# Linear attention and a four-expert mixture: less work for the last 64 tokens and keys, finer steps, a new order

## The chip, the cores and the metric

The kernel runs on one core of one Trainium2 chip. The metric is the device time of one launch in microseconds (us). Within a core five engines run from queues of their own: TensorE (PE; its weight loads are shown as PEld), VectorE (DVE), ScalarE (ACT), GpSimd (POOL), and SyncE (SP), which here issues the DMA transfers. An engine takes its instructions in the order in which the program lists them.

## The reference

Inputs are q, k and v of 8 batches, 8 heads, 576 positions and 64 features, a feature matrix w_phi, and the weights of four experts. First linear attention, for each batch and head:

```
proj = x @ w_phi                                   (128 features)
proj = proj - max |proj| over the features
phi(x) = [exp(proj), exp(-proj)]                   (256 features)
kv = phi(k)^T @ v,   z = sum over positions of phi(k)
attn = (phi(q) @ kv) / (phi(q) . z + 1e-6)
```

The eight heads side by side give x, 576 by 512 for each batch. Then four experts, each a causal softmax attention of one head of 64 features:

```
logits = x @ w_gate;  the two largest of four experts per token, softmax over these two
for each expert: q, k, v = x @ wq, x @ wk, x @ wv
                 ye = softmax_causal(q k^T / 8) @ v @ wo
                 out += gate * ye
```

576 is 4 times 128 and 64: every stage over positions has four full blocks and a tail of 64.

## The kernel before

Heads go in 32 pairs, four pairs to a batch. Each pair passes through these stages of the first part:

- stream_k projects the keys (8 products of 128 columns) and stream_tail the last 64 keys of both heads together (2 products with 64 weight columns each); center takes the maximum over the features and subtracts it on VectorE, and ScalarE takes both exponentials into ek.
- stream_kv multiplies ek with v (40 products: 2 heads, 2 halves of the features, 5 blocks of keys, 2 halves of the output rows). A column of ones beside v gives z. The last 64 keys of the two heads share one block, 64 rows for each head, and v has zeros in the other head's rows.
- stream_q projects the queries; phi_q takes the maximum over the features with a GpSimd all-reduce, subtracts it on VectorE and takes both exponentials on ScalarE.
- stream_n multiplies phi(q) with kv (72 instructions of 65 columns per pair), normed divides, turn_x transposes by a 32x32 VectorE transpose and a trip through DRAM. The result is split into a high and a low part in fp32r, xh and xl (sub_lo on VectorE).

The second part, stream_b, takes a batch when the x of its four pairs is there. Products with weights are three fp32r products each (high-high, high-low, low-high). proj_t makes queries and keys of two experts at a time (g = 0, 1), each in two pieces of 256 and 320 positions; proj_v makes the values and gate logits in five blocks of positions, 12 products of 260 columns each; scores makes the scores in four groups (BLOCKS), soft masks and evicts them, post takes the maximum over keys (GpSimd) and the exponential, then multiplies with the values; norm_y divides and applies the gate, move_y transposes (turn_y on TensorE in the last batch), project_out multiplies with wo and store writes.

A plain f32 product is two instructions on TensorE, an fp32r product one. TensorE sees three tile shapes: 128x128 (products with wqk, wvg, wo), 64x128 (q and k projections, scores) and 128x64 (key tail, kv, phi(q) kv, attention times values).

Every stage is a Python generator that yields a Step before each group of instructions, with the engine and a condition (pred) on what must have been issued. The order of all steps on all engines is written out in PICKS: two characters per step, which generator goes next and which of the 8 PSUM banks it gets, or for an eviction whether ScalarE or VectorE does it. in_order then keeps each engine's queue in that order. So an engine never passes over an instruction that waits. Before the change, ORDER fixed the order of a batch's stages (all of p0, then v0, and so on), each stage being one long generator, and keep_warm issued three small bf16 products on a tile of ones whenever PICKS put it in, until the first x was there: 126 in all.

## Time and profile before

| | |
|---|---|
| time, three runs | 565.3 us median (564.62, 565.3, 569.82) |
| profiled execution | span 563.5 us from the first to the last instruction; its time is not listed apart, the span is 1.8 us under the median and 1.1 us under the fastest run |
| TensorE busy | 551.8 us, 98% |
| TensorE weight loads busy | 518.7 us, 92% |
| VectorE busy | 492.9 us, 87% |
| ScalarE busy | 391.2 us, 69% |
| GpSimd busy | 192.7 us, 34% |
| DMA queues | 48.7% of the 16 engines' span, 123 GB/s of HBM traffic |
| granted TensorE clock | 0.999 on average |

Busy time is the union of the instructions of an engine, and pipelined instructions overlap; for TensorE the distance from one start to the next tells more than the duration of one. The chain that ended last goes through TensorE for 88% of the span and through VectorE for 8%.

### The profile page before, as it was taken

Reading aid. Unit: us, or ns where it says so; the run is one execution under the profiler, and the core shown is the slowest. Engines: PE = TensorE matmul, PEld = TensorE weight load, DVE = VectorE, ACT = ScalarE, POOL = GpSimd, SP = SyncE. Lnnn points to the kernel's source line nnn. Section 1 sums busy time; section 2 is a strip of 40 time slices with the busy share of each in tenths; the row PEclk is TensorE's granted clock in tenths of the full one; section 3 lists DMA queues with packets and bytes.
Section 4 is the critical chain, followed back from the end, with each engine's and each line's share of the span. In section 5 each row is a group of like instructions: output and inputs, shape, how many; then the busy total and the mean of one; then the engine's idle time right before and its main releaser. Section 6 shows DMA issues by size and latency. Waiting matters only on the chain.

```text
span 563.5 us, 22862 instructions
## 1 busy us (share of the span) xinstructions
PE 551.8 (98%) x9704; PEld 518.7 (92%) x9704; DVE 492.9 (87%) x1245; ACT 391.2 (69%) x737; POOL 192.7 (34%) x78
## 2 busy tenths in 40 slices
PE   8999899999999999999999999999999999999996
PEld 6888799999999999999999999999999999999996
DVE  5799988999998999898878998899988998896992
ACT  3978757877956666897755784877785865574673
POOL 4565082244220555233203525083522310202320
PEclk9999999999999999999999999999999999999999
DMA  6577655555554636526545644356553253414222
GB/s 169 145 186 200 171 153 118 154 124 122 150 133 102 181 87 177 140 71 180 126 93 141 163 144 98 85 136 170 141 112 65 62 134 80 112 47 105 66 85 85
DMA packets 124757, 70.63 MB, mean 125 GB/s; under 512 B 81520, under 2 KB 107504, under 8 KB 124656
## 3 DMA queue, kind: packets, MB, share of 16 engines
q1 hardware_dynamic: 124656, 69.18, 48.7%
q8 instruction: 76, 1.25, 1.0%
q14 instruction: 25, 0.20, 0.1%
HBM read 46.15 MB, written 23.00 MB: 123 GB/s over the span
## 4 chain that ended last, share of the span: by engine, by line
PE 88%; DVE 8%; ACT 2%; issue 1%; DMA 0%; SPq 0%; DVEq 0%; ACTq 0%
PE ps_c L180 39%; PE ps_c L407 30%; PE ps_c L359 11%; PE ps_c L626 7%; DVE st L744 1%; DVE pmax L393 1%; DVE ek L395 1%; ACT ek L191 1%; DVE u L508 1%; DMA wf<-in_wts_dram 0%; DVE xt L540 0%; DVE xq L438 0%; DVE kv L202 0%; ACT u L189 0%; DVE u L202 0%
## 5 line engine op out<-in xcount | busy, mean ns | idle before, releaser
L498 POOL PARTITION_ALL_REDUCE mx<-u x32 | 127.0, 3993 | 113.7 <-ACT u L189 74.3
L180 PE MATMUL ps_c<-xh,qk 128*128 128x320 f32 (+1 forms) x512 | 106.3, 299 | 0.2 <-ACT st L189 0.2
L191 ACT ACTIVATE ek<-ek 128x1152 f32<-128x1152 f32 x64 | 74.8, 1169 | 26.4 <-DVE ek L395 25.5
L180 PEld LDWEIGHTS ps_c<-xh,qk 128*128 128x128 f32 x512 | 83.2, 189 | 1.8 <-ACT st L189 0.5
L498 POOL PARTITION_ALL_REDUCE tops<-top x15 | 54.2, 3611 | 82.9 <-DVE top L658 70.5
L407 PEld LDWEIGHTS ps_c<-v_in,ek 128*64 128x64 f32 x2560 | 77.4, 137 | 5.1 <-issue 2.6
L407 PE MATMUL ps_c<-v_in,ek 128*64 128x65 f32 x2560 | 81.4, 222 | 0.5 <-ACT ek L191 0.4
L180 PE MATMUL ps_c<-xl,qk 128*128 128x256 f32 (+1 forms) x256 | 75.8, 296 | 0.0
L189 ACT COPY st<-ps_c 128x288 f32<-128x288 f32 (+1 forms) x120 | 51.4, 505 | 25.1 <-DVE ps_c L646 16.7
L407 PE MATMUL ps_c<-kv,mx 128*64 128x65 f32 x1152 | 62.5, 224 | 3.3 <-DVE kv L202 2.6
L744 DVE TENSOR_TENSOR st<-st,tops 128x1152 f32<-128x1152 f32 (+4 forms) x75 | 57.7, 826 | 4.5 <-POOL tops L498 4.4
L393 DVE TENSOR_REDUCE pmax<-ps_c 128x4 f32<-128x512 f32 (+1 forms) x96 | 51.1, 546 | 11.0 <-PE ps_c L407 5.6
L407 PE MATMUL ps_c<-kv,u 128*64 128x65 f32 x1152 | 59.5, 221 | 0.0
L180 PE MATMUL ps_c<-vg,xh 128*128 128x260 f32 (+1 forms) x320 | 59.0, 285 | 0.0
L407 PEld LDWEIGHTS ps_c<-kv,mx 128*64 128x64 f32 x1152 | 48.1, 137 | 8.0 <-DVE kv L202 1.9
L189 ACT COPY u<-ps_c 128x320 f32<-128x320 f32 (+3 forms) x125 | 42.6, 416 | 17.2 <-PE ps_c L359 15.2
L395 DVE TENSOR_TENSOR ek<-ps_c,pmax 128x512 f32<-128x512 f32 (+1 forms) x96 | 51.9, 553 | 2.8 <-issue 0.5
L191 ACT ACTIVATE st<-st 128x1152 f32<-128x1152 f32 (+3 forms) x60 | 48.5, 865 | 7.0 <-DVE st L744 6.6
L180 PE MATMUL ps_c<-yh,wo 128*128 128x256 f32 (+1 forms) x256 | 52.1, 298 | 0.0
L180 PEld LDWEIGHTS ps_c<-xl,qk 128*128 128x128 f32 x256 | 48.5, 189 | 0.1
L407 PE MATMUL ps_c<-vl,st 128*64 128x65 f32 x1500 | 47.6, 222 | 0.8 <-ACT st L191 0.7
L180 PEld LDWEIGHTS ps_c<-vg,xh 128*128 128x128 f32 (+1 forms) x320 | 47.6, 177 | 0.8 <-issue 0.3
(116 smaller groups left out, 1175.4 us busy)
## 6 DMA issues: line engine op xcount, KB each, us to landing
v_in<-in_v_dram SPq DMA_DIRECT2D x32, 320.0 KB, 4.1
q_in<-in_qt_dram SPq DMA_DIRECT2D x64, 144.0 KB, 3.5
xl<-xd SPq DMA_DIRECT2D x32, 288.0 KB, 3.1
out_dram<-ot SPq DMA_DIRECT2D x32, 288.0 KB, 2.9
k_in<-in_kt_dram SPq DMA_DIRECT2D x32, 160.0 KB, 3.4
xd<-xt SPq DMA_DIRECT2D x64, 80.0 KB, 2.5
k_in<-in_kt_dram SPq DMA_DIRECT2D x32, 128.0 KB, 3.3
xd<-xt SPq DMA_DIRECT2D x64, 64.0 KB, 2.1
```

What stands on the lines that cost most here:

```text
L180: nc.tensor.matmul(o, a, b, start=start, stop=stop, skip_group_check=True)
L189: nc.scalar.copy(o, i)
L191: nc.scalar.activation(o, i, func, **kw)
L359: nc.tensor.matmul(o, a, b, start=True, stop=True, skip_group_check=True)
L393: dve(n * 128, [mk], [pk]).tensor_reduce(out=m[:, us], in_=src, axis=AX.X, op=ALU.max, apply_absolute_value=True)
L395: dve(n * 128, [(f'ek{p % EKB}1', us.start)], [pk, mk]).tensor_tensor(out=ek2[p % EKB][:, 1, us, :], in0=src, in1=m[:, us].unsqueeze(2).to ...
L407: nc.tensor.matmul(o, a, b, start=start, stop=stop, skip_group_check=True)
L498: nc.gpsimd.partition_all_reduce(o, i, 128, op)
L508: dve(2 * S, [uk], [mk], port=True).tensor_tensor(out=U, in0=U, in1=M, op=ALU.subtract)
L626: nc.tensor.matmul(pp_[e][:, o:o + q1 - q0], kk2[k_][r, 128 * j:128 * j + 128], q2[q_][r, q0:q1], start=m == 0, stop=m == 2, skip_group_ch ...
L744: dve(2 * n, [sj[j]], [*key, mk], port=True).tensor_tensor(out=a, in0=a, in1=tops[x][0:m, :, 128 * j:], op=ALU.subtract)
```

## The change

The values of the last 64 tokens: after its split, 64 columns of xh and 64 of xl are copied by a DMA side by side into xE, and proj_v's last block takes these 128 columns as weights, with high and low wvg (8 products; low times low comes along). Its two output halves are added: a copy to vlo, then an addition on VectorE. The last 64 keys in stream_kv: one product for both heads, 130 columns. The last score block has 64 weight columns in place of 128, and the memsets of the padding go.

The steps become finer: each piece of proj_t, each block of proj_v and each piece of project_out is a generator of its own; stream_kv and stream_n run through one half of the features and then the other, and may start after the first exponential; attention times values (attend) goes block of queries by block of queries as the exponentials come, and no longer waits for the gate, which norm_y does; in the last batch project_out may take g = 0 first. The warm products are 18 groups of three, 54, and the first four key projections wait for 8, 12, 15 and 18 groups. PICKS is a new table for all steps. Before the change TensorE has 6024 products in the program, after it 5792.

```diff
-WARM = 0
-ORDER = (('p0', 'v0', 's0', 'p1', 's1'), ('p0', 's0', 'p1', 's1', 'v0'))
+WARMS = 18
+WARM_AT = (7, 11, 14, 17)
...
-    "BACACADAAAAAAAAAAAAAAAAAAAGRNANAGjNANANACAG1OAOAG5OAOAOABAAAFCPIPIEjQIPIPIPIEADANICACAAAAAAAAAAAAAAAAAAAAAAAAAAAAAG1PAPA"
...
+    "BABABABABADABABABABAAAAAAAAAGIGaBANADAEsRACANARANANAFGBANAAHAHQAAHAHAHAHOAFHFRQAOANANADADADrBAFGGAEEMAMATANIJHJAJANIOAPA"
...
+    nc.vector.memset(warm, 1.0)
-        nc.vector.memset(t[:, NJ * V1 - 1:NJ * V1], 0.0)
+        nc.vector.memset(t[:, NJ * V1 - 1:512], 0.0)
...
-    xT = [[sb(f"x{p}{i}", [128, S], F32R) for p in "hl"] for i in range(PXB)]
+    xB = [sb(f"xb{i}", [128, 2, S], F32R) for i in range(PXB)]
+    xT = [[t[:, n] for n in range(2)] for t in xB]
+    xE = sb("xe", [128, NP, 128], F32R)
...
-    kk2 = [sb(f"kk{p}", [128, KC], F32R) for p in "hl"]
+    kk2 = [sb(f"kk{p}", [128, S], F32R) for p in "hl"]
+    vlo = sb("vlo", [64, 4, 65])
...
     def keep_warm():
-        pk, ps = yield Step('PE', (), 'c')
-        while ('x', WARM, 0) not in done:
-            yield Step('PE')
+        for n in range(WARMS):
+            t = yield Step('PE', (), 'c')
             for _ in range(3):
-                mm(ps[:, 0:128], warm, warm, True, True, 128, pk, [])
-        plan.release('c', (pk, ps))
+                mm(t[1][:, 0:128], warm, warm, True, True, 128, t[0], [])
+            plan.release('c', t)
+            done.add(('warm', n))
...
             x, need = k_in[p % IB], [(f'k_in{p % IB}', n) for n in range(2)] + ['wphi']
-            k0, k1, pp_ = yield Step('PE', need, 'c', lambda: ('load_k', p) in done and ('w', 0) in done, tiling=(64, 128), n=3)
...
             i = p % EKB
             ek, ekk = ek2[i], [f'ek{i}0'] + [(f'ek{i}1', t) for t in (0, 4, 8)]
-            kc, ps = yield Step('PE', ekk + [vk], 'c', lambda: ('phi_k', p) in done and ('load_v', p) in done, tiling=(128, 64))
-            for h in range(2):
-                for c in range(2):
+            kc, ps = yield Step('PE', ekk + [vk], 'c', lambda: ('phi_k', p, 0) in done and ('load_v', p) in done, tiling=(128, 64))
+            for c in range(2):
+                if c:
+                    yield Step('PE', pred=has('phi_k', p, 1))
+                for h in range(2):
                     o = V1 * (2 * h + c)
-                    for t in range(NJ):
-                        u_ = 4 * h + t if t < 4 else 8
+                    for t in range(4):
                         for m in range(0, 128, 64):
-                            column_mm(ps[m:m + 64, o:o + V1], ek[:, c, u_, m:m + 64], v_in[:, 4 * h + t if t < 4 else 8 + h, :],
-                                       t == 0, t == 4, kc, ekk + [vk])
+                            column_mm(ps[m:m + 64, o:o + V1], ek[:, c, 4 * h + t, m:m + 64], v_in[:, 4 * h + t, :], c + h + t == 0, False, kc, ekk + [vk])
...
             kvi = kv[p % 2]
-            k0, k1, pp_ = yield Step('PE', need, 'c', lambda: ('phi', p) in done and ('kvs', p) in done, tiling=(128, 64), n=3)
-            for j in range(NJ):
-                for c in range(2):
-                    rows_mm(j, pp_, (k0, k1), lambda h, m: P_[h][c][:, 64 * j + 5 * m:], lambda h: kvi[:, 2 * h + c, :], c == 0, c == 1, need)
+            k0, k1, pp_ = yield Step('PE', need, 'c', lambda: ('phi', p, 0) in done and ('kvs', p) in done, tiling=(128, 64), n=3)
+            for c in range(2):
+                if c:
+                    yield Step('PE', pred=has('phi', p, 1))
+                for j in range(NJ):
+                    rows_mm(j, pp_, (k0, k1), lambda h, m: P_[h][c][:, 64 * j + 5 * m:], lambda h: kvi[:, 2 * h + c, :], c + j == 0, c == 1, need)
             done.add(('num', p))
             plan.spawn(divide(p, (k0, k1), pp_))
             plan.spawn(turn_x(p))
...
+        yield Step('SP', [f'xl{i}'], pred=(lambda: ('pe', p // NP - 1) in done) if p >= NP else None)
+        load(xE[:, p % NP].rearrange("f (n s) -> f n s", n=2).bitcast(F32), xB[i][:, :, 512:S].bitcast(F32), 'xe')
+        done.add(('xe', p))
...
-        def proj_t(sel, g):
+        def proj_t(b, sel, g, s0, s1):
             w = wsp["qk"]
-            for s0, s1 in PARTS:
-                pk, ps = yield Step('PE', [k for c in xk for k in c], 'c')
-                n = 0
-                for c in range(4):
-                    o = ((sel * 4 + c) * 2 + g) * 128
-                    for w_, x_ in ((0, 0), (0, 1), (1, 0)):
-                        mm(ps[:, 0:s1 - s0], w[w_][:, o:o + 128], xs[c][x_][:, s0:s1],
-                           n == 0, n == 11, s1 - s0, pk, [xk[c][x_], ('qk', w_)])
-                        n += 1
-                plan.spawn((evac_k if sel else evac_q)(g, s0, s1, pk, ps))
+            pk, ps = yield Step('PE', (), 'c', ready_x)
+            n = 0
+            for c in range(4):
+                o = ((sel * 4 + c) * 2 + g) * 128
+                for w_, x_ in ((0, 0), (0, 1), (1, 0)):
+                    mm(ps[:, 0:s1 - s0], w[w_][:, o:o + 128], xs[c][x_][:, s0:s1], n == 0, n == 11, s1 - s0, pk, [])
+                    n += 1
+            plan.spawn((evac_k if sel else evac_q)(g, s0, s1, pk, ps))
+            used()
+
+        def used():
+            left[0] -= 1
+            if left[0] == 0:
+                done.add(('px', b))
...
-            copy(st.eng, 260, vl[:m, j, :, 0:65], ps[:m, 0:260].rearrange("p (n d) -> p n d", d=65), [f'vs{j}'], [kc])
+            src = ps[:, 0:260].rearrange("p (n d) -> p n d", d=65)
+            if m == 128:
+                copy(st.eng, 260, vl[:, j, :, 0:65], src, [f'vs{j}'], [kc])
+            else:
+                copy(st.eng, 260, vlo, src[64:128], ['vlo'], [kc])
+                yield Step('DVE', [kc], hot=True)
+                nc.vector.tensor_tensor(out=vl[0:64, j, :, 0:65], in0=src[0:64], in1=vlo, op=ALU.add)
...
-                            nc.tensor.matmul(pp_[e][:, o:o + q1 - q0], kk2[k_][r, 128 * j:128 * j + 128], q2[q_][r, q0:q1],
+                            n_ = min(128, S - 128 * j)
+                            nc.tensor.matmul(pp_[e][0:n_, o:o + q1 - q0], kk2[k_][r, 128 * j:128 * j + n_], q2[q_][r, q0:q1],
...
+            plan.spawn(attend(b, g))
...
-        def proj_v():
+        def proj_v(j):
             wvg = wsp["vg"]
-            for j in range(NJ):
-                m = min(128, S - 128 * j)
-                kc, ps = yield Step('PE', [k for c in xk for k in c], 'c', has('av', b - 1, 1) if b else has('w', 2))
-                n = 0
-                for c in range(4):
-                    for x_, w_ in ((0, 0), (0, 1), (1, 0)):
-                        mm(ps[:m, 0:260], xs[c][x_][:, 128 * j:128 * j + m],
-                           wvg[w_][:, c * 260:(c + 1) * 260], n == 0, n == 11, 260, kc,
-                           [xk[c][x_], ('vg', w_)])
-                        n += 1
-                plan.spawn(evac_v(j, m, kc, ps))
-
-        yield Step('PE', (), None, lambda: all_x(*range(b * NP, b * NP + NP))() and all(('w', i) in done for i in (0, 1, 4)))
-        for part in ORDER[b == B - 1]:
-            yield Step('PE')
-            g = int(part[-1])
-            if part[0] == 'p':
-                yield from proj_t(0, g)
-                yield from proj_t(1, g)
-            elif part[0] == 'v':
-                yield from proj_v()
-                plan.spawn(gates(b))
-            else:
-                yield from scores(g)
-            if part == ORDER[b == B - 1][-1]:
-                plan.spawn(project_out(b))
-            if part in 'p1v0' and part == [o for o in ORDER[b == B - 1] if o[0] in 'pv'][-1]:
-                done.add(('px', b))
+            m = min(128, S - 128 * j)
+            kc, ps = yield Step('PE', (), 'c', lambda: ready_x() and ('w', 2) in done and (j < NJ - 1 or all(('xe', NP * b + c) in done for c in range(NP))))
+            parts = [(xs[c][x_][:, 128 * j:128 * j + m], c, w_) for c in range(4) for x_, w_ in ((0, 0), (0, 1), (1, 0))]
+            if m < 128:
+                parts = [(xE[:, c], c, w_) for c in range(4) for w_ in range(2)]
+            for n, (x_, c, w_) in enumerate(parts):
+                mm(ps[:, 0:260], x_, wvg[w_][:, c * 260:(c + 1) * 260], n == 0, n == len(parts) - 1, 260, kc, [])
+            if m < 128:
+                done.add(('pe', b))
+            plan.spawn(evac_v(j, m, kc, ps))
+            used()
...
+        left = [13]
+        yield Step('PE', (), None, all_x(b * NP))
+        for g in range(2):
+            for sel in range(2):
+                for s0, s1 in PARTS:
+                    plan.spawn(proj_t(b, sel, g, s0, s1))
+        for j in range(NJ):
+            plan.spawn(proj_v(j))
+        plan.spawn(gates(b))
+        for g in range(2):
+            plan.spawn(scores(g))
+        for t in range(4):
+            for s0, s1 in PARTS:
+                plan.spawn(project_out(b, t, s0, s1))
+            plan.spawn(store(b, t))
...
-        for j in range(NJ):
-            done.add(('e', b, g, j))
+            for j in js:
+                done.add(('e', b, g, j))
...
         def ready():
-            return all(('v', b, j) in done for j in range(NJ)) and ('gate', b) in done
+            return all(('v', b, j) in done for j in range(NJ)) and ('e', b, g, 0) in done
 
         k0, k1, pp_ = yield Step('PE', ej[0:1], 'c', ready, tiling=(128, 64), n=3)
         for i in range(NJ):
+            if i:
+                yield Step('PE', pred=has('e', b, g, i))
...
-        yield Step('DVE', pred=(lambda: all(('yt', b - 1, g, q_[0]) in done for q_ in PARTS)) if b else None)
+        yield Step('DVE', pred=lambda: ('gate', b) in done and (not b or all(('yt', b - 1, g, q_[0]) in done for q_ in PARTS)))
...
+        early = b == B - 1
+        pk, ps = yield Step('PE', (), 'c', lambda: ('w', 3) in done and ys_done(b, 0) and (early or ys_done(b, 1)))
+        for g in range(2):
+            if g and early:
+                yield Step('PE', pred=lambda: ys_done(b, 1))
+            wc = slice(512 * g + 128 * t, 512 * g + 128 * t + 128)
+            for n, (y_, w_) in enumerate(((0, 0), (0, 1), (1, 0))):
+                mm(ps[:, 0:s1 - s0], wwo[w_][:, wc], ys[g][y_][:, s0:s1], g == 0 and n == 0, g == 1 and n == 2, s1 - s0, pk, [])
+        plan.spawn(evac_o(b, t, s0, s1, pk, ps))
+        todo[b] -= 1
+        if todo[b] == 0:
+            done.add(('o', b))
```

What PICKS moves is seen in the built order. First TensorE at the value tail of a batch (vg are the value and gate weights; xh and xl, or xe, hold x; ps is PSUM), before:

```order
L180 MATMUL ps_c_61<-vg,xh_152 128x260 x2
L180 MATMUL ps_c_61<-vg,xl_153 128x260
L180 MATMUL ps_c_66<-vg,xh_146 64x260 x2
L180 MATMUL ps_c_66<-vg,xl_147 64x260
L180 MATMUL ps_c_66<-vg,xh_148 64x260 x2
L180 MATMUL ps_c_66<-vg,xl_149 64x260
L180 MATMUL ps_c_66<-vg,xh_150 64x260 x2
L180 MATMUL ps_c_66<-vg,xl_151 64x260
L180 MATMUL ps_c_66<-vg,xh_152 64x260 x2
L180 MATMUL ps_c_66<-vg,xl_153 64x260
L626 MATMUL ps_c_67<-qh,kkh 128x288
```

and in the change, where it follows the second query and key projection (qk):

```order
L184 MATMUL ps_c_68<-xb_148,qk 128x256 x3
L184 MATMUL ps_c_68<-xb_149,qk 128x256 x3
L184 MATMUL ps_c_65<-vg,xe 128x260 x8
L184 MATMUL ps_c_66<-vg,xb_146 128x260 x3
L184 MATMUL ps_c_66<-vg,xb_147 128x260 x3
```

Twelve products with 64 output rows became eight with 128, and they now stand ahead of other value blocks.

Second, TensorE at the end of the program: the last attention (vl are the values, u a buffer of exponentials), the transposes (ident, yq) and the output products (yh, yl, wo), before:

```order
L407 MATMUL ps_c_66<-vl,u_127 64x65
L407 MATMUL ps_c_68<-vl,u_127 64x65
L450 MATMUL ps_c_63<-ident,yq_165 128x128 x2
L450 MATMUL ps_c_67<-ident,yq_165 128x128 x2
L450 MATMUL ps_c_67<-ident,yq_165 128x64
L450 MATMUL ps_c_64<-ident,yq_166 128x128 x2
```

and in the change:

```order
L407 MATMUL ps_c_63<-vl,u_127 64x65
L407 MATMUL ps_c_62<-vl,u_127 64x65
L184 MATMUL ps_c_64<-yh_180,wo 128x320 x2
L184 MATMUL ps_c_64<-yl_181,wo 128x320
L184 MATMUL ps_c_64<-yh_182,wo 128x320 x2
L184 MATMUL ps_c_64<-yl_183,wo 128x320
L184 MATMUL ps_c_66<-yh_180,wo 128x256 x2
L184 MATMUL ps_c_66<-yl_181,wo 128x256
L184 MATMUL ps_c_66<-yh_182,wo 128x256 x2
L184 MATMUL ps_c_66<-yl_183,wo 128x256
L450 MATMUL ps_c_67<-ident,yq_160 128x128 x2
```

Twelve output products of the batch before now stand between the last attention and the transposes.

Third, VectorE in the opening, where the x of the first batch is split (xl and xh before, xb in the change; qk and vg are pieces of the weights, rd, xq and xt belong to the division and transpose of other pairs), before:

```order
L185 TENSOR_TENSOR xl_153<-xl_153,xh_152 128x576
L444 TENSOR_SCALAR xq_137<-ps_c_65,rd_135 64x2x32
L185 TENSOR_TENSOR qk<-ot_188,qk 128x576
L202 COPY kv_122<-ps_c_64 128x260
L540 STREAM_TRANSPOSE xt_142<-xq_136 128x640
L185 TENSOR_TENSOR xl_151<-xl_151,xh_150 128x576
L202 CAST vg<-ot_189 128x4x64 x2
```

and in the change:

```order
L206 CAST xb_148<-xb_148 128x576
L206 CAST xb_147<-xb_147 128x576
L189 TENSOR_TENSOR xb_148<-xb_148 128x576
L189 TENSOR_TENSOR xb_146<-xb_146 128x576
L393 TENSOR_REDUCE pmax_124<-ps_c_62 128x1
L438 TENSOR_TENSOR xq_136<-ps_c_63,rd_134 128x4x2x32
L189 TENSOR_TENSOR xb_147<-xb_147 128x576
L189 TENSOR_TENSOR xb_149<-xb_149 128x576
L395 TENSOR_TENSOR ek_119<-ps_c_62,pmax_124 128x128
L546 STREAM_TRANSPOSE xt_142<-xq_136 128x640
```

The four subtractions stand together now, with two of the casts just ahead of them on the same engine, and the last weight pieces behind them.

## Rows read from the trace of the kernel before

**Rows 1.** Windows by stage: window, length, busy us (count) by engine, clock, DMA.

```profile
0.00:30.00 30.00, 27.55 (x479) 23.23 (x481) 20.35 (x73) 17.98 (x28) 16.17 (x10) 1.00 0.61 160
30.00:74.40 44.40, 41.69 (x962) 36.29 (x961) 43.35 (x96) 35.36 (x58) 18.53 (x5) 1.00 0.69 181
74.40:540.00 465.60, 463.30 (x7973) 441.10 (x7974) 416.61 (x1042) 326.90 (x626) 154.22 (x63) 1.00 0.48 119
540.00:563.50 23.50, 19.25 (x296) 18.10 (x294) 12.61 (x35) 10.95 (x26) 3.74 (x2) 0.98 0.27 102
```

**Rows 2.** Waits of TensorE from 75 us: us in total, times, longest (five rows).

```profile
PE ps_c L450 <- DVE yq L438: 0.8, 1, 0.8
...
PE ps_c L407 <- ACT st L191: 0.7, 2, 0.5
...
PE ps_c L180 <- ACT st L189: 0.2, 1, 0.2
```

**Rows 3.** Chain that ended last, 515 to 565 us: start, us, what.

```profile
544.93 6.04 PE ps_c L407 x200
...
552.49 0.86 PE ps_c L450 x5
```

**Rows 4.** TensorE in order of time: start, us, what; a value tail and a score tail.

```profile
86.45 0.29 PE L180 MATMUL ps_c<-vg,xl 128*128 128x260 f32 x1
86.58 0.40 PE L180 MATMUL ps_c<-vg,xh 128*64 128x260 f32 x2
...
87.89 0.28 PE L180 MATMUL ps_c<-vg,xl 128*64 128x260 f32 x1
88.09 0.40 PE L626 MATMUL ps_c<-qh,kkh 64*128 64x288 f32 x2
...
89.59 0.19 PE L626 MATMUL ps_c<-qh,kkh 64*128 64x64 f32 x2
...
89.84 0.39 PE L626 MATMUL ps_c<-qh,kkh 64*128 64x320 f32 x2
```

**Rows 5.** TensorE in order of time, where the tile shape changes at 202 us.

```profile
202.16 0.29 PE L407 MATMUL ps_c<-kv,u 128*64 128x65 f32 x4
202.38 0.70 PE L359 MATMUL ps_c<-q_in,wf 64*128 64x256 f32 x4
```

**Rows 6.** TensorE in order of time: kv products, and a key tail at 110 us.

```profile
98.65 2.56 PE L407 MATMUL ps_c<-v_in,ek 128*64 128x65 f32 x80
101.04 0.39 PE L407 MATMUL ps_c<-wf,k_in 128*64 128x128 f32 x4
...
110.36 0.29 PE L407 MATMUL ps_c<-kv,u 128*64 128x65 f32 x4
110.48 0.39 PE L407 MATMUL ps_c<-wf,k_in 128*64 128x128 f32 x4
110.70 1.51 PE L407 MATMUL ps_c<-vl,st 128*64 128x65 f32 x46
```

**Rows 7.** Waits of VectorE, 75 to 540 us (fifteen rows, first and last).

```profile
DVE ps_c L646 <- PE ps_c L626: 6.4, 7, 2.0
...
DVE ek L395 <- PE ps_c L407: 0.2, 1, 0.2
```

**Rows 8.** Forms on VectorE: busy us, mean ns of one, idle before.

```profile
L202 DVE COPY kv<-ps_c 128x260 f32<-128x260 f32 x8 | 3.4, 422 | 0.5 <-PE ps_c L407 0.4
L202 DVE COPY u<-ps_c 128x320 f32<-128x320 f32 x5 | 2.2, 483 | 0.3 <-PE ps_c L359 0.3
L202 DVE CAST xh<-xl 128x576 fp32r<-128x576 f32 x3 | 1.6, 527 | 0.0
```

**Rows 9.** TensorE in order of time: warm products in the opening.

```profile
1.30 2.74 PE L180 MATMUL ps_c<-warm 128*128 128x128 bf16 x24 [1.30 <-DVE col L215]
...
10.98 2.52 PE L180 MATMUL ps_c<-warm 128*128 128x128 bf16 x42
```

More of the change, by code (lines that the diff above doesn't have):

```diff
@@ L169, in tile_linear_attn_moe @@
     plan.free = set(range(BANKS))
+    warm = cp.tile([128, 128], BF16, name="warm")
+    nc.vector.memset(warm, 1.0)
     for t in plan.both:
-        nc.vector.memset(t[:, NJ * V1 - 1:NJ * V1], 0.0)
+        nc.vector.memset(t[:, NJ * V1 - 1:512], 0.0)
     def sb(name, shape, dt=F32):
@@ L363, in stream_k @@
             x, need = k_in[p % IB], [(f'k_in{p % IB}', n) for n in range(2)] + ['wphi']
-            k0, k1, pp_ = yield Step('PE', need, 'c', lambda: ('load_k', p) in done and ('w', 0) in done, tiling=(64, 128), n=3)
+            k0, k1, pp_ = yield Step('PE', need, 'c', lambda: ('load_k', p) in done and ('w', 0) in done and (p >= len(WARM_AT) or ('warm', WARM_AT[p]) in done), tiling=(64, 128), n=3)
             for n in range(4):
@@ new lines, in proj_v, with has_scores, ready_x @@
+            if m < 128:
+                done.add(('pe', b))
+            plan.spawn(evac_v(j, m, kc, ps))
+            used()
+        def has_scores(g):
+            return has('s', b, 0) if g else (has('s', b - 1, 1) if b else None)
+        def ready_x():
+            return all_x(*range(b * NP, b * NP + NP))() and ('w', 1) in done
+        left = [13]
[4 more added lines that the diff above has]
+                    plan.spawn(proj_t(b, sel, g, s0, s1))
```

136 lines of the change are left out of this document (63 added, 73 removed).

## The prediction

> **What bounds the kernel now.** I read the busy time by stage first. From the first query and key product at 74.4 us to 540 us TensorE is busy 463.3 of 465.6 us [rows 1]; in that stretch and the tail behind it only 2.7 us of its waits have a name, in five rows [rows 2]. A busy TensorE can still be slow, so I looked at start-to-start times next: the twelve products of a tail follow each other 0.12 us apart [rows 4], and 80 small products take 2.39 us [rows 6], without holes. From 74.4 us on, then, the time is the sum of TensorE's own work, and less of that work is less time as long as nobody else falls behind. Three things are not that sum. The opening, up to 74.4 us: from 30 us VectorE is busy 43.35 of 44.4 us there, TensorE 41.7 [rows 1]. The end: attention ends at 544.93 + 6.04 = 550.97 us and the transposes start at 552.49, 1.5 us of TensorE waiting for the division [rows 3]. And VectorE's own load: 416.6 of 465.6 us in the steady part [rows 1], second in the queue to be the bound.
>
> The span is 563.5 us; the median of the runs is 565.3. I work on the span and add 1.8 us.
>
> **The change, part by part.** TensorE first.
>
> Value products of the last 64 tokens: 12 of them per batch become 8 (the weights now hold the high and the low part side by side). Eleven steps take 87.89 - 86.58 = 1.31 us, 0.119 each [rows 4]; all stream 260 columns before and after. 8 batches x 4 x 0.119 = 3.8 us. The new copy of those 64 columns (one DMA of 64 KB for each of 32 pairs) and the wait for it I cost at nothing on TensorE: in the order of batch 0 two query and key projections lie between the fourth x subtraction and the product that reads it, 96 products of 0.12 us or more, over 11 us. If that cover is gone, SP's queue is where it hurts, since loads stand behind the waiting copy.
>
> Key products of the last 64 keys: 16 instructions of 65 columns per pair of heads become 8 of 130 (each f32 product is two instructions). Now: 16 x 2.39/80 = 0.48 us. For 130 columns the nearest row has 128: four in 0.22 us, 0.055 each [rows 6], so 8 x 0.056 = 0.45. 32 pairs x 0.03 = 1.0 us saved. Bounds: 0, and 7.7 us if an instruction of 130 columns cost no more than one of 65; the row of 128 columns says it does not.
>
> Score block of the last 64 keys: the same six products of 64 columns, with 64 weight columns for 128. Six take 0.25 us, 16 times 4.0 us in all [rows 4]. I take 0; bounds are a gain of half, 2.0 us, and a loss of 3.0 (below).
>
> Changes of the tile shape. Between stages of the same shape the next one follows at its normal distance: four products to the next stage 0.12 us [rows 6]. Into another shape the same four need 0.22 [rows 5], and value to scores 0.20 where 0.12 is normal [rows 4]. So a change costs 0.08 to 0.11; I take 0.095. In the order I count the changes behind the first query/key product, the narrow value and score products put with their neighbours: 115 before, 74 now. 41 x 0.095 = 3.9 us (3.3 to 4.5).
>
> The end: 12 output products of the batch before now stand between the last attention and the transposes, 1.6 us of work in a hole of 1.5. The hole goes: 1.5 us.
>
> Opening. VectorE sets it, so I count what its queue holds ahead of the fourth x subtraction. Leaving: six kv copies of 0.42 us [rows 8], three u copies, one subtraction and one transpose, and smaller ones, 8.3 us; joining: three casts of x of 0.53 [rows 8], k-side reductions and subtractions, weight casts, 4.5 us. 3.8 us less, at 0.89 (below) 3.4. The first k projection also moves ahead of the second q projection, and VectorE gets its first work sooner: it idles 9.65 us before 30 us [rows 1]; I take 1.2. But 1.6 us of useful TensorE work also moves from the opening to behind it. Net 3.0 us. Bounds: a loss of 1 (the second q load is issued later), a gain of 8. The 72 warm products that go (0.06 us each [rows 9], 4.3 us) and 18 shape changes are inside this: they filled time in which VectorE was the bound.
>
> TensorE's sum: 563.5 - 3.8 - 1.0 - 3.9 - 1.5 - 3.0 = 550.3 us of span, 552.1 in time.
>
> Now VectorE, which the order loads more: 22 score evictions, 13 output evictions, 13 u copies, 8 casts of x and 10 value evictions come over from ScalarE, and each batch adds one 64x260 addition for the value tail. By 0.48 us for 320 columns, 0.42 for 260, 0.53 for a cast [rows 8] and in proportion for other widths: 12.2 + 5.9 + 5.7 + 4.2 + 4.2 + 3.4 and 1.3 of small ones, 36.9 us; kv copies and small products of the division go to ScalarE, -7.4. 29.5 us of durations. Neighbours overlap (492.9 us busy for 551.6 us of durations, count by mean over the forms, 0.89), so 26 us busy: 492.9 + 26 = 519. Its idle time: 10.7 us up to 74.4, of which I let 2 go; 49.0 in the steady part [rows 1], of which 34.3 are waits in fifteen rows [rows 7] and 14.7 small gaps; 10.9 at the end, less the hole of 1.5. With no wait left: 519 + 8.7 + 14.7 + 9.4 = 551.8 us of span, 553.6 in time. That the waits go under load is what the stretch from 30 to 74.4 us shows: full queue, 1.05 us idle in 44.4.
>
> So the two sums nearly meet, at 552.1 and 553.6. Two engines that are both full now and then wait for each other; I add 1.4 us. Forecast **555 us**, 1.8% faster. The half steps (TensorE may begin on the first exponential) I cost at nothing: TensorE's queue is in order, a second half that waits holds up all behind it, and there was 0.7 us of waiting for exponentials to win [rows 2].
>
> A rule of the Trainium skill speaks against the score tail. Those products go from tiles of 64x128 to 64x64 and back, 32 changes more. The rows nearest to it: the value tail narrowed its weights from 128 to 64 columns, and its first product came 0.13 us after the one before, against 0.12 within [rows 4]: no price. The Trainium skill, "TensorEngine Tiling (Array Packing)", section Tiling Modes, says that changing the tiling mode drains TensorE. By that rule all 32 changes would cost the 0.095 us of the other changes, 3.0 us, and the TensorE sum would be 555.1; the trace agrees with it for the three shapes of the kernel and not for the narrow value products.
>
> **The rivals.**
> (1) VectorE carries the end. For: the two sums differ by 1.5 us, and evictions that it does late keep banks from TensorE. If half of the 21.9 us that it waits for ScalarE, GpSimd and issue stays, 553.6 + 11 = 565 us: no change. Against: the 30 to 74.4 us stretch. Chance 0.17.
> (2) The same chain to its end, slower: all 34.3 us of waits stay beside the new evictions in the steady part, 553.6 + 34.3 = 588 us. It is slower by over 1% from the point where 17 of the 34 stay. Against: 12.4 of these are waits for TensorE, which cost nothing when TensorE is ahead. Chance 0.05.
> (3) The narrow score tiles cost a change each: TensorE then sums to 555.1, clearly above VectorE, 558 us with the same 1.4 and a little more of waiting. Chance 0.12.
> (4) The opening falls to the lower clock. The first 24 warm products take 2.74 us, 114 ns each, the 42 at 10.98 us 60 ns [rows 9]; the 72 that go stood between 11 and 36 us. If TensorE runs there at 1.2 GHz, the 20 us that it is busy up to 30 us without the warm products [rows 1] become 40, and VectorE's idle time there takes 8 of them: 555 + 12 = 567 us. Against: the granted clock is 1.00, 2.4 GHz, in all stretches up to 540 us [rows 1], and the opening keeps real products every few us. Chance 0.04.
> (5) It goes better: the opening gains 8 us rather than 3, and VectorE's gaps shrink to the share they have from 30 to 74.4 us (2.4% of 465.6, 11 us for 14.7). 555 - 5 - 4 = 546 us. Chance 0.15.
> That the change does less than it says is not among them: products, counts and shapes stand in the built order.
>
> **How the numbers follow.** The forecast has 0.47, the rivals 0.17, 0.05, 0.12, 0.04 and 0.15. Its own range, by the bounds of the terms, is 550 to 560. The range for all reaches down to (5), 546, and up past (1), 566; left out are the lowest third of (5), (2), (4) and the upper third of (1), 0.2 together. A measurement of this kernel can tell 1%, 5.7 us: faster means under 559.6. Faster: nearly all of the forecast (0.44), two thirds of (3) (0.08), (5) (0.15), and the lucky part of (1) (0.03): 0.70. Slower (over 571): 0.05. The rest, 0.25, is no change.
>
> **What the profile would show.** Right: 54 warm products; the first query/key product at 69 to 72 us; eight value tail products in 0.95 us and no group of 12; distances of 0.056 us at the 130-column products; no hole before the last transposes; VectorE over 92% busy, ScalarE under 68%; TensorE over 98% still. Wrong: score tails with 0.1 us at either side (3); TensorE's waits after 75 us summing to over 10 us on evictions or masks that VectorE does (1, 2); SP's copies of the 64 columns as what TensorE waits for. The forecast fails first if VectorE's queue, with 26 us more in it, is late at the banks.

## The result, and the profile after

| | kernel before | changed kernel |
|---|---|---|
| time, median of 13 runs | 565.8 us | 561.3 us (555.7 to 567.7) |
| ratio | | 0.9892, 95% interval 0.9862 to 0.9923 |
| profiled execution | span 563.5 us | span 558.0 us, time 559.8 us |
| mean granted TensorE clock | 0.999 | 0.993 |

1.1% faster, where 1.8% was forecast. The ratio is taken over the runs and not from the two medians, whose quotient is 0.992: five of the 13 runs of the kernel before took 567 to 570 us, and the one run of the changed kernel that took 567.7 us is left out. The median is 6.3 us over the forecast of 555; the profiled execution was 1.5 us faster than the median, and its span is 4.8 us over the 553.2 that the forecast meant. The busy times of the page, and the stages that answer to [rows 1]; the columns are those of that group:

```profile
PE 536.5 (96%) x9344; PEld 510.5 (91%) x9344; DVE 501.7 (90%) x1299; ACT 374.7 (67%) x691; POOL 193.4 (35%) x76
```

```profile
30.00:74.40 44.40, 41.10 (x894) 38.48 (x891) 38.08 (x92) 35.11 (x62) 20.48 (x6) 0.96 0.72 189
74.40:540.00 465.60, 455.34 (x7844) 436.92 (x7844) 432.30 (x1099) 315.05 (x586) 159.12 (x63) 1.00 0.50 122
```

In the steady stretch TensorE is now idle for 10.3 us, not 2.3, and VectorE for 33.3, not 49.0. The first query/key product, before and after:

```profile
74.29 0.38 PE L180 MATMUL ps_c<-xh,qk 128*128 128x256 f32 x1
```

```profile
66.96 3.21 PE L184 MATMUL ps_c<-xb,qk 128*128 128x320 f32 x22
```

So the whole gain of this execution is made in the opening, 7.3 us; from that product to the end the span has 491.0 us, where it had 489.2, in spite of the work that went. Behind the first query/key product the waits of TensorE that answer to [rows 2] are these twelve (total, times, longest); they sum to 10.9 us, and no one cause leads:

```profile
PE ps_c L407 <- issue: 2.1, 4, 0.9
PE ps_c L358 <- DVE xq L444: 1.6, 1, 1.6
PE ps_c L358 <- ACT vl L193: 1.6, 1, 1.6
PE ps_c L184 <- DVE yl L832: 1.0, 1, 1.0
...
PE ps_c L407 <- ACT st L195: 0.2, 1, 0.2
```

The product work itself came out as planned, in TensorE's order of time (a key tail; a score tail; a value tail and the change of tile shape behind it; the end):

```profile
22.73 0.39 PE L468 MATMUL ps_c<-v_in,ek 128*64 128x130 f32 x4
22.95 1.22 PE L407 MATMUL ps_c<-kv,mx 128*64 128x65 f32 x36
...
112.90 0.37 PE L646 MATMUL ps_c<-ql,kkh 64*128 64x448 f32 x2
113.10 0.20 PE L646 MATMUL ps_c<-qh,kkh 64*64 64x64 f32 x2
...
113.24 0.40 PE L646 MATMUL ps_c<-qh,kkh 64*128 64x320 f32 x2
...
343.23 1.11 PE L184 MATMUL ps_c<-vg,xe 128*128 128x260 f32 x8
344.18 3.02 PE L184 MATMUL ps_c<-vg,xb 128*128 128x260 f32 x24
347.13 0.40 PE L646 MATMUL ps_c<-qh,kkh 64*128 64x288 f32 x2
...
543.99 0.28 PE L184 MATMUL ps_c<-yl,wo 128*128 128x256 f32 x1
544.35 0.71 PE L450 MATMUL ps_c<-ident,yq 128*128 128x128 f32 x4
```

Eight products in 344.18 - 343.23 = 0.95 us; four of 130 columns in 0.22. The six narrow score products take 113.24 - 113.10 = 0.14 us, where [rows 4] had 0.25, with nothing lost at either side. The 24 value products take 347.13 - 344.18 = 2.95 us to the next tile shape, 0.09 over 24 steps of 0.119: a change among the old three shapes costs what it did. The hole ahead of the last transposes is gone.

Two holes show what was new. The first is in the opening. SP's queue, TensorE, the stages of 2 and 1 us there (columns as in [rows 1]; the clock is the third from the right), and a piece of the chain of waits (start, us, what):

```profile
45.51 2.94 SPq L214 DMA_DIRECT2D xd<-xt  x4
48.50 1.39 SPq L214 DMA_DIRECT2D v_in<-in_v_dram  x2
```

```profile
53.77 1.15 PE L407 MATMUL ps_c<-v_in,ek 128*64 128x65 f32 x32 [3.30 <-DMA v_in<-in_v_dram]
54.72 0.57 PE L468 MATMUL ps_c<-v_in,ek 128*64 128x130 f32 x4
55.01 2.01 PE L407 MATMUL ps_c<-v_in,ek 128*64 128x65 f32 x32
```

```profile
50.00:52.00 2.00, 0.47 (x17) 0.33 (x12) 1.97 (x4) 1.39 (x4) 2.00 (x1) 1.00 1.07 243
52.00:54.00 2.00, 0.23 (x8) 0.27 (x9) 1.93 (x7) 1.66 (x2) 1.86 (x1) 1.00 0.89 192
...
55.00:56.00 1.00, 1.00 (x23) 1.00 (x21) 1.00 (x5) 0.00 (x0) 0.00 (x0) 0.50 0.78 193
...
57.00:58.00 1.00, 1.00 (x7) 0.56 (x5) 0.00 (x0) 0.00 (x0) 0.00 (x0) 0.50 0.83 191
```

```profile
48.50 5.13 DMA v_in<-in_v_dram
```

The v_in load stands behind four writes of x, whose issue keeps SP from 45.51 to 48.45 us, and lands 5.13 us after its own issue (the median is 4.5). TensorE is idle for 3.3 us, and then the granted clock is 0.50 (1.2 GHz): the same 32 products take 2.01 us, not 1.10. So this hole is paid twice. The second is at 348 us, told by the chain of waits, TensorE's row and three stages:

```profile
340.29 6.76 DMA xb<-xd
347.05 0.02 issue
347.07 0.04 DVE xb L206
...
347.45 1.36 DVE u L511
...
348.84 1.16 ACT mx L195
350.00 0.54 ACT vl L193 x2
```

```profile
350.32 0.48 PE L358 MATMUL ps_c<-q_in,wf 64*128 64x256 f32 x1 [1.56 <-ACT vl L193]
```

```profile
340.00:345.00 5.00, 5.00 (x42) 5.00 (x42) 0.75 (x3) 3.79 (x7) 0.59 (x1) 1.00 0.94 218
...
348.00:350.00 2.00, 0.76 (x6) 0.27 (x2) 1.97 (x3) 1.16 (x2) 0.00 (x0) 1.00 0.32 121
...
352.00:354.00 2.00, 2.00 (x20) 2.00 (x21) 1.93 (x5) 0.59 (x3) 0.00 (x0) 0.50 0.48 101
```

A load of x takes 6.8 us (the median is 3.3); the DMA engines are 94% busy in its first five us, but 6% from 346 to 347, when it has still not landed. A cast of x, now on VectorE, waits for it at the head of VectorE's queue (0.75 us busy of 5). Behind the cast stand the subtraction of phi_q, the exponential on ScalarE that needs it, and two value evictions that free TensorE's bank: TensorE is idle for 1.6 us, and again the clock falls. Not every hole is followed by that: one of 1.6 us at 307 us, where TensorE waits for VectorE's xq, has a clock of 1.00 in the stages of 5 us from 305 to 315. The transfers of x from issue to landing, before and after:

```profile
DMA to landing us min/median/max: 1.7/2.8/4.8
```

```profile
DMA to landing us min/median/max: 1.7/2.6/7.1
```

### The profile page after: what moved, and what is told of

Read it like the earlier page. It is cut to its first block, busy times and chain, and to the rows that moved or that the text cites. A ratio compares the mean times of both kernels' runs of the same rounds, so it can differ in the third digit from the quotient of the medians.

```text
span 558.0 us, 22167 instructions
## 1 busy us (share of the span) xinstructions
PE 536.5 (96%) x9344; PEld 510.5 (91%) x9344; DVE 501.7 (90%) x1299; ACT 374.7 (67%) x691; POOL 193.4 (35%) x76
## 4 chain that ended last, share of the span: by engine, by line
PE 75%; DVE 10%; DMA 5%; SPq 5%; issue 2%; ACT 2%; DVEq 0%; ACTq 0%
PE ps_c L184 30%; PE ps_c L407 26%; PE ps_c L358 10%; PE ps_c L646 6%; SPq L214 5%; PE ps_c L468 2%; DVE st L770 2%; DMA v_in<-in_v_dram 1%; DMA xb<-xd 1%; DVE pmax L393 1%; DVE u L511 1%; DMA q_in<-in_qt_dram 1%; DMA xd<-xt 1%; DVE ek L395 1%; DVE top L679 1%
## 5 line engine op out<-in xcount | busy, mean ns | idle before, releaser
L184 PE MATMUL ps_c<-xb,qk 128*128 128x256 f32 (+1 forms) x768 | 107.6, 296 | 0.7 <-DVE top L679 0.7
L184 PEld LDWEIGHTS ps_c<-xb,qk 128*128 128x128 f32 x768 | 103.2, 188 | 1.8 <-ACT st L193 0.9
L184 PE MATMUL ps_c<-yh,wo 128*128 128x320 f32 (+1 forms) x256 | 53.2, 300 | 0.2 <-DMA v_in<-in_v_dram 0.2
L184 PE MATMUL ps_c<-vg,xb 128*128 128x260 f32 x384 | 50.3, 284 | 0.0
L407 PEld LDWEIGHTS ps_c<-vl,st 128*64 128x64 f32 x1500 | 47.0, 138 | 2.0 <-ACT ot L193 1.0
L184 PEld LDWEIGHTS ps_c<-vg,xb 128*128 128x128 f32 x384 | 47.7, 188 | 0.7 <-issue 0.5
L358 PE MATMUL ps_c<-q_in,wf 64*128 64x320 f32 (+1 forms) x256 | 44.4, 434 | 3.4 <-DVE xq L444 1.6
L511 DVE TENSOR_TENSOR u<-u,mx 128x1152 f32<-128x1152 f32 x32 | 44.7, 1400 | 1.1 <-POOL mx L501 0.9
L195 ACT ACTIVATE mx<-u 128x1152 f32<-128x1152 f32 x32 | 37.4, 1169 | 7.6 <-DVE u L511 7.6
L184 PEld LDWEIGHTS ps_c<-yh,wo 128*128 128x128 f32 x256 | 40.7, 188 | 1.5 <-DVE ek L395 0.4
```

What stands on the lines that cost most here:

```text
L184: nc.tensor.matmul(o, a, b, start=start, stop=stop, skip_group_check=True)
L195: nc.scalar.activation(o, i, func, **kw)
L358: nc.tensor.matmul(o, a, b, start=True, stop=True, skip_group_check=True)
L407: nc.tensor.matmul(o, a, b, start=start, stop=stop, skip_group_check=True)
L511: dve(2 * S, [uk], [mk], port=True).tensor_tensor(out=U, in0=U, in1=M, op=ALU.subtract)
```

## The experiments

Times of twelve kernels, each against the kernel before on its own chip; the last column is the mean granted clock of the runs:

| run | median us | ratio, 95% interval | clock |
|---|---|---|---|
| after_again | 559.3 | 0.9883 (0.9847 to 0.9919) | 0.992 |
| before_fewer | 561.4 | 0.9946 (0.9912 to 0.9979) | 0.999 |
| tails_full | 558.6 | 0.9870 (0.9838 to 0.9902) | 0.996 |
| v5_early | 558.2 | 0.9880 (0.9836 to 0.9924) | 0.994 |
| casts_act | 559.5 | 0.9887 (0.9853 to 0.9920) | 0.992 |
| pe_less | 555.2 | 0.9813 (0.9774 to 0.9853) | 0.989 |
| dve_less | 556.2 | 0.9818 (0.9778 to 0.9859) | 0.993 |
| both_less | 555.9 | 0.9824 (0.9781 to 0.9866) | 0.990 |
| before_less | 592.4 | 1.0460 (1.0417 to 1.0502) | 0.979 |
| sp_less | 562.8 | 0.9950 (0.9917 to 0.9982) | 0.993 |
| both_sp_less | 556.8 | 0.9829 (0.9775 to 0.9882) | 0.986 |
| fillers | 557.2 | 0.9868 (0.9829 to 0.9907) | 0.997 |

**The measure.** The changed kernel again, on the chip of tails_full, v5_early and casts_act.

> The changed kernel itself, as the measure for the three that follow. Both theories: ratio to the kernel before 0.989 (0.986 to 0.992), first query/key product at 67 us, TensorE idle 3.3 us at the v_in load near 50 us.

The ratio was as expected, the hole was not: in this profile TensorE waits 3.9 us ahead of the first query/key product instead, and the clock falls at three places (65 to 75, 355 to 365, 545 to 550 us). The chain of waits has a load of x there too, of 4.83 us, ahead of its cast on ScalarE. Where the holes fall differs between the two profiles of this kernel; that there are some does not.

**The product work, in either order.** In the old order the products alone, with nothing added for them:

```diff
-                    for x_, w_ in ((0, 0), (0, 1), (1, 0)):
+                    for x_, w_ in ((0, 0), (0, 1), (1, 0))[:3 if m == 128 else 2]:
...
```

> The kernel before, in its own order and with no work added anywhere: the value tails leave out the four products with the low part of x (eight of twelve remain), the key tails are one product of 130 columns. TensorE has 4.8 us less by the terms of the prediction. Theory (in that order TensorE sets the pace, and the product work is worth its time): 4 to 5.5 us faster, ratio 0.990 to 0.993. Rival (hidden, TensorE waits in its place): ratio 0.996 to 1.001.

0.54% of 565.2 is 3.1 us (1.2 to 5.0): the theory's 4.8 lies inside, but the ratio lies between the two ranges, 0.0016 from the theory's and 0.0014 from the rival's. The profile speaks for the theory: the span fell 4.3 us, TensorE's busy time 5.2, its clock stayed at 0.999. Then the same work put back into the new order:

```diff
-                parts = [(xE[:, c], c, w_) for c in range(4) for w_ in range(2)]
+                parts = [(xs[c][x_][:, 512:S], c, w_) for c in range(4) for x_, w_ in ((0, 0), (0, 1), (1, 0))]
...
```

> The changed kernel in its own order, but the value tails have twelve products of 64 columns again (no copies of the 64 columns, no addition on VectorE) and the key tails two products of 65 columns per pair and half; the score tails stay narrow. Theory (TensorE's sum holds, the two terms are worth 4.8 us): 4 to 5 us slower than the changed kernel, ratio 0.997 (0.995 to 1.000). Rival (where TensorE waits for others anyway the products are hidden, and the 32 copies in SP's queue cost something of their own): 0 to 2.5 us slower, ratio 0.989 to 0.993.

It is no slower at all, and both ranges miss. So in the new order the tails, with the copies and additions that they bring, gain nothing: the longer products can fill time in which TensorE would wait, the clock is at 0.996 for 0.992, and 32 copies and eight additions are saved. How much of the 4.8 us each of these takes was not separated.

**Two late places, mended one at a time.** The v_in load of the sixth pair is issued ahead of the x transfers:

```diff
...
+            if who == ('turn_x', 0) and ('xw', 0) in self.done and ('load_v', 5) not in self.done:
...
+                self.advance(v, None)          # load_v's next step now, and not at its own place
...
```

> The changed kernel, one load moved: SP issues the v_in load of the sixth pair ahead of the first xd read and the four xd writes of the second pair, all else in the same order. Theory (the late load costs): the 3.3 us in which TensorE waits for v_in near 50 us goes, and with it the granted clock of 0.67 from 55 to 60 us; 32 kv products take 1.1 us there, not 2.0; the first query/key product comes at 62 us, not 67, and the ratio to the kernel before falls from 0.989 to 0.980 (0.978 to 0.983). Rival (VectorE's chain to the x subtractions sets the opening): TensorE's idle time only moves to another wait, the first query/key product stays at 66 to 67 us and the ratio within 0.002 of the changed kernel.

The load came 3.8 us earlier, at 44.67 us, the clock stayed at 1.00 up to 65 us, and the first query/key product came later, not sooner (in an execution of 562.2 us, where the median is 558.2):

```profile
52.86 1.16 PE L417 MATMUL ps_c<-v_in,ek 128*64 128x65 f32 x32 [2.39 <-DVE ek L405]
...
69.19 3.12 PE L194 MATMUL ps_c<-xb,qk 128*128 128x320 f32 x11 [4.64 <-ACT xq L205]
```

```profile
61.66 6.45 DMA xb<-xd
...
68.14 0.67 ACT xb L203
...
68.83 0.32 ACT xq L205
...
69.19 0.45 PE ps_c L194
```

The wait moved to VectorE's ek and then, by the chain of waits (second fence), to the same kind of place as at 348 us: a load of x takes 6.45 us, its cast, here on ScalarE, stands at the head of the queue, and the last piece of a division behind it frees TensorE's bank late. The rival was right that the gain goes, but of the 7.0 us of waits VectorE's ek has 2.4 and the chain of x through DRAM 4.6. Next, the casts that had waited at the head of VectorE's queue:

```diff
-        copy(st_.eng, S, hi, lo.bitcast(F32), [f'xh{i}'], xr, 0.52)
+        copy('ACT', S, hi, lo.bitcast(F32), [f'xh{i}'], xr, 0.52)
```

> The changed kernel, all 32 casts of x on ScalarE (11 or so of them are on VectorE). Theory (what stands in VectorE's queue behind a cast that waits for its DMA is what TensorE waits for): VectorE's waits for the DMA of xb, 8.2 us of which 6.3 in one, go; TensorE's waits behind 75 us fall from 11 to 6 or 7 us and the ratio from 0.989 to 0.982 (0.979 to 0.985). Rival (VectorE's load as such, or the place of the loads in SP's queue): ScalarE's copies now stand behind the same casts, TensorE's waits stay at 10 us or over with other names, ratio 0.987 to 0.992.

No gain: the rival. VectorE's waits for the loads of x are gone, but TensorE's named waits behind 75 us still sum to 10.6 us, the longest now 1.9 us for a score eviction on ScalarE, which stands behind a cast and a load of x of 4.37 us. What is late there is the data, and either engine hands the delay on.

**Load taken off each engine.** These kernels leave out part of the result, to see what the time does.

```diff
-  parts = [... for x_, w_ in ((0, 0), (0, 1), (1, 0))]
+  parts = [... for x_, w_ in ((0, 0), (0, 1), (1, 0))[:2 if m == 128 else 3]]      # pe_less, both_less
...
+        if p % 3 == 2:                                                              # dve_less, both_less
             sub_lo(S, lo, lo.bitcast(F32), hi, f'xl{i}', [*xr, f'xh{i}'])
```

> The changed kernel with 15.4 us of TensorE work less: the value products of the first 512 tokens leave out the product with the low part of x (128 products of 0.12 us). Theory (VectorE sets the pace in this order): 0 to 3 us faster than the changed kernel, ratio 0.983 to 0.989, TensorE's waits grow by 12 us or more. Rival (TensorE sets it): 12 to 15 us faster, ratio 0.962 to 0.968. Third (neither alone, each holds the other): 5 to 8 us, ratio 0.975 to 0.980.

> The changed kernel with 16 us of VectorE work less: 22 of the 32 subtractions that make the low part of x are left out (0.74 us each). Theory (VectorE sets the pace): 9 to 15 us faster than the changed kernel, ratio 0.963 to 0.973, TensorE's waits behind 75 us gone. Rival (TensorE sets it): 0 to 3 us faster, 0.983 to 0.989. Third (each holds the other): 5 to 8 us, 0.975 to 0.980.

> The changed kernel with both left out, 15.4 us of TensorE and 16 us of VectorE work. Theory (VectorE) and its rival (TensorE) alike: 13 to 17 us faster than the changed kernel, ratio 0.958 to 0.966. Third (each holds the other): the sum of the two single gains or more, 0.958 to 0.966. If it is under 8 us faster (0.975 and over), neither engine's load sets the pace but the loads and copies through SP's queue or waits between the two.

15.4 us off TensorE gave about 4 us, 16 us off VectorE about 4, both together no more: 561.3 or 559.3 to 555 or 556. Each gain has some 3 us of uncertainty, by the intervals of the two ratios behind it. All three forecasts of the single runs miss (each lies between two of them), and the last clause of the expectation for both holds, clear of the noise: neither engine's load sets the pace. The chain of waits from 75 to 540 us shows what takes over, by line, in the kernel before, the changed one and both_less:

```profile
by line: PE ps_c L180 43.7%; PE ps_c L407 30.8%; PE ps_c L359 9.8%; PE ps_c L626 8.7%; DVE st L744 1.6%; DVE pmax L393 0.6%; DVE ek L395 0.6%; ACT ek L191 0.5%; issue 0.4%; DVE u L508 0.3%; DVE gs L725 0.3%; DVE xq L438 0.3%; DVE gw L723 0.
```

```profile
by line: PE ps_c L184 33.2%; PE ps_c L407 26.1%; PE ps_c L358 9.1%; PE ps_c L646 7.3%; SPq L214 4.2%; issue 2.0%; PE ps_c L468 1.9%; DVE st L770 1.8%; DMA xb<-xd 1.5%; DVE u L511 1.2%; DMA xd<-xt 0.9%; DVE top L679 0.9%; DVE u L770 0.8%; DV
```

```profile
by line: PE ps_c L184 26.3%; PE ps_c L407 17.4%; PE ps_c L358 6.9%; PE ps_c L647 6.7%; DVE st L771 3.9%; SPq L214 3.4%; issue 3.4%; DMA xd<-xt 2.5%; DVE u L511 1.8%; DVE top L680 1.7%; DMA xb<-xd 1.6%; DVE pmax L393 1.6%; ACT mx L195 1.4%; 
```

TensorE's lines that are listed sum to 93% of the chain, then 78%, then 57%: the rest goes over to many short pieces of VectorE, ScalarE, SP and transfers.

**SP's queue.** It is a third place that could set the pace. First the product work as the change has it, in the old order, the copy put straight behind the subtraction:

```diff
...
+        load(xE[p // NP % 2][:, p % NP].rearrange("f (n s) -> f n s", n=2).bitcast(F32), xB[i][:, :, 512:S].bitcast(F32), 'xe')
         for s0, s1 in PARTS:
             done.add(('x', p, s0))
...
```

> The kernel before, in its own order, with the product work of the change alone: value tails of eight products (the 64 columns copied by SP behind the subtraction, the two halves added on VectorE), key tails of one product of 130 columns, narrow score tails. In that order TensorE had no waits: theory (product work is worth its TensorE time where TensorE sets the pace, and nothing in the order of the change, where VectorE's order sets it): 4 to 5 us faster than the kernel before, ratio 0.992 (0.990 to 0.995). Rival (the products are hidden there too, or the copies in SP's queue cost it): ratio 0.997 to 1.003.

26 us slower, missed by both. SP's queue, 75 to 540 us (what it waits for: total, times, longest):

```profile
SPq L210 <- DVE xb L185: 39.8, 9, 11.3
```

SP stands nine times for 39.8 us at a copy until VectorE has subtracted, and the loads behind are late: TensorE waits 4.2 us for v_in, 3.0 for q_in, and its clock falls to 0.979 on average. The additions stand on VectorE straight behind ScalarE's copy, for another 6.7 us, so the 26 us are not the copies' alone. In the changed kernel the copies are well placed: SP's one wait at them is 1.4 us. Then SP relieved, in the new order:

```diff
-        load(xE[:, p % NP]..., 'xe')
+        nc.gpsimd.tensor_copy(xE[:, p % NP]..., xB[i][:, :, 512:S].bitcast(F32))
...
-        load(out[b, 128 * t:128 * t + 128, :], ot[t % 2], ('out', b, t), oks)
+        nc.scalar.dma_start(out[b, 128 * t:128 * t + 128, :], ot[t % 2])
```

> The changed kernel with 64 of SP's 385 transfers taken out of its queue: the 32 copies of the last 64 columns of x are made by GpSimd on the chip (no transfer), the 32 output stores are issued by ScalarE. Theory (SP's queue in order is what holds the pace: it stands 54 us before output stores, and the loads behind them come late): 3 to 6 us faster than the changed kernel, ratio to the kernel before 0.979 to 0.984. Rival (the waits between TensorE, VectorE, ScalarE and GpSimd hold it, whatever the queue does): within 2 us of the changed kernel, 0.986 to 0.992.

> The same with the value products and the subtractions of both_less left out too (15.4 us of TensorE, 16 us of VectorE). Theory (SP's queue): with the queue relieved the less work counts, 6 to 11 us faster than both_less, ratio 0.963 to 0.972. Rival (waits between the engines, in the fixed order): ratio 0.978 to 0.985, as both_less.

The theory is not borne out. sp_less is 3 to 4 us slower than the changed kernel, outside the rival's range too: ScalarE and VectorE now wait 17.9 us for stores out of their buffers (7.9 before the move), GpSimd is busy 15 us more, so the relief brought waits of its own. With the load off as well it stands where both_less stood, as the rival said. That SP's queue has no part is not shown by this.

**The clock.** Warm products ahead of four places that had shown holes:

```diff
+    def fill(ps, n):
+        for _ in range(n):
+            mm(ps[:, 384:512], warm, warm, True, True, 128, None, [])
...
+            fill(ps, 30 if p == 5 else 0)          # stream_kv; stream_n p 6, stream_q and stream_tail p 26 alike
```

> The changed kernel with 108 warm products more (0.056 us each, 6.0 us together) into unused columns of a bank, at the four places at which runs of it have shown holes of 2 to 4 us on TensorE: 30 ahead of the first kv product of the sixth pair (which waits for v_in near 50 us), 30 behind the numerators of the seventh pair (ahead of the first query/key product), 24 behind the first half of the 27th query projection (348 us), 24 behind the 27th key tail (357 us). Theory (holes of 3 us cost a second time, since the granted clock falls to 1.2 GHz behind them: 4.1 us of clock in the changed kernel's profile against 0.4 before): clock lost falls under 1.5 us, the holes cost no more than without, 2 to 3.5 us faster than the changed kernel, ratio 0.983 to 0.986. Rival (the fillers delay TensorE wherever there is no hole, or the holes move): the clock is lost elsewhere or the 6 us are paid, ratio 0.988 to 0.997.

The mechanism held at its place: the hole is cut in two, and the products behind it run at full speed.

```profile
50.56 1.83 PE L184 MATMUL ps_c<-warm 128*128 128x128 bf16 x30 [1.10 <-DVE ek L400]
53.55 1.16 PE L412 MATMUL ps_c<-v_in,ek 128*64 128x65 f32 x32 [1.15 <-DMA v_in<-in_v_dram]
54.53 0.39 PE L474 MATMUL ps_c<-v_in,ek 128*64 128x130 f32 x4
54.75 1.10 PE L412 MATMUL ps_c<-v_in,ek 128*64 128x65 f32 x32
```

The clock is 1.00 in all stages of this profile and 0.997 over the runs. The time is 557.2 us, between the two expectations: 0.15 to 0.24% under the changed kernel, inside the intervals. It has the lowest median of the kernels that compute all of the reference, and is not shown to be faster than the change.

## Why the prediction was right, and what it missed

The direction and the range (546 to 566) held; the size was 6.3 us of time too good, 4.8 us of the profiled span. The range held by its width: 561.3 us lies outside the forecast's own 550 to 560 and inside only because the range was drawn past rival (1). By the prediction's line for faster, under 559.6 us, the median is no change; by the ratio, 1.1% (0.8 to 1.4), the gain lies on that line of 1%.

Most of the terms came true, and what they save is not seen in the time. In both profiles of the changed kernel the gain is the opening alone, and the stretch behind it, for which the terms of TensorE's sum say some 8 us less (3.8, 1.0, 3.9 and 1.5, less the 1.6 that moved there), is 1.8 us longer (1.5 in after_again).

- **Value and key tails:** as forecast, 0.95 us for eight, 0.055 us per step at 130 columns; worth 3.1 us (1.2 to 5.0) in the old order for the 4.8 forecast; with their copies and additions, nothing in the new.
- **Score tail:** taken at 0, it gained 0.11 us 16 times, 1.8 us, near its bound. Rival (3) is out. The Trainium skill, "TensorEngine Tiling (Array Packing)", section Tiling Modes, has TensorE drained when the mode changes; no such price shows between 64x128 and 64x64 here.
- **Tile shapes:** as forecast: counted in the traces as the prediction counts, 115 changes before and 74 after, and one still costs 0.09 us.
- **Opening:** better than forecast: the first query/key product came at 66.96 us, 7.3 earlier (3.0 + 1.6 = 4.6 was forecast), though v_in cost a hole of 3.3 us and, at a clock of 0.67 from 55 to 60 us, 1.65 more. SP's queue was named for the copies; that the x writes would stand ahead of a v_in load was not seen. Rival (4) came true in small, by this hole and not by the warm products that went.
- **End:** the hole of 1.5 us went, and 0.6 us of waits are left. But from the end of the last product to the end of the span it is 4.6 us, where it was 3.5: two evictions follow each other on ScalarE there, where one stood.
- **VectorE:** 519 us busy were forecast, 501.7 came: the durations rose from 551.6 to 572.9 us, by 21.4 and not 29.5, and 12.6 of these lie beside other work of VectorE. It is at 90%, not over 92%; TensorE is at 96%, not over 98%.
- **The failed step:** "Two engines that are both full now and then wait for each other; I add 1.4 us." The overlap of the two engines was mis-sized. TensorE's own sum was 550.3 us of span, and the forecast allowed 2.9 us over it, 1.5 up to VectorE's sum and the 1.4; the span is 558.0, 7.7 over it. TensorE's waits behind the first query/key product are 10.9 us, where the forecast left 1.9 (2.7 less the 0.8 that go with the hole at the end), and the clock that fell behind the hole at 348 us (0.68 from 350 to 355 us) cost 1.6 us: 9.0 + 1.6 - 2.7 (opening) - 1.8 (score tail) = 6.1 of the 7.7 us. Of the 1.6 left, 1.1 stand behind the last product. Waits of over 10 us were the sign for the rivals (1) and (2), but on VectorE's work; here TensorE waits 4.0 us for VectorE, 4.6 for ScalarE, 2.1 for nothing that the profile shows and 0.2 for a load. VectorE's load is not their cause, since 16 us less of it gave 4. The rule behind the forecast, that the time is the larger of two engines' sums, fits the old order (before_fewer) and not the new one, where less work on either or both gives about a quarter or less.

What stays open: which loop of waits sets the pace once TensorE's sum no longer does, and why some loads of x land late. The trip of x through DRAM stands at four holes whose chains were followed (at 348 us, and in after_again, v5_early and casts_act), so it is the first suspect; it was only argued from these chains, since no run took it away. The v_in load, the casts, the output stores and the copies of the 64 columns were moved without gain; the all-reduces and the number of buffers were not tried.

## What to carry to other kernels

When one engine is busy for over 99% of a stretch and a change takes its work away, count on the sum only as far as the next chains, here a quarter of a per cent away by the forecast's own two sums; then expect a fraction or nothing, and measure it by taking load off each engine in turn. Look for a transfer that waits ahead of loads in the same queue: SP stood 40 us at such transfers in the kernel that lost 26, with other waits beside them. Look also for a cast that waits for a load ahead of evictions, but moving the cast to another engine gained nothing here, as the load stayed late. And count a hole on TensorE with what the clock may take behind it. Last, split the gain at a landmark such as the first query/key product: it shows which part of the kernel the gain comes from.

## What the runs showed of the hardware

- A hole of 3.3 us was followed by a granted clock of 0.50; filled with 1.8 us of warm products, with 1.1 us idle on either side, by 1.00. The Trainium skill, "TensorE: Matmul & The Clock Gate", section Loop structure matters more than you think, says that a long wait for a DMA between every two matmuls lets TensorE go cold; here a single such wait of 3.3 us was followed by it, with 2.01 us for 1.10. The length of a hole alone does not tell: one of 1.6 us at 348 us was followed by 0.50, one of 1.6 us at 307 us and v5_early's of 2.39 us by 1.00. Over 13 runs the change has a mean clock of 0.993; the profile of the kernel before has 0.999.
- A score block of 64x64 tiles after 64x128 ones cost no change, and its six products went from 0.25 to 0.14 us.
- The same 288 KB read of x took 3.3 us at the median, but 6.8 us in one flight in which the DMA engines were 77% busy on average, 6.45 in one of 79% (v5_early) and 4.83 in one of 90% (after_again). So their busy share does not tell when it lands.
